# K of the second attention transposed in place, in one ring of eight tiles, in a two-attention kernel on one Trainium2 core

## The chip, the cores and the metric

The kernel runs on one core of one Trainium2 chip. The core has a matrix engine (PE, whose weight loads are listed apart as PEld), a vector engine (DVE), an engine for activations (ACT), a general one (POOL) and a sequencer (SP) that issues all transfers here. 16 DMA engines move the data between device memory and the on-chip memory, which has 128 partitions. Engines run their own instructions in order and wait for each other through semaphores. The metric is the time of one execution on the device in microseconds (us); lower is better.

## What is computed

Two attention blocks, A and B, over the same shapes of x (16 sequences of 32 tokens, width 1024; all data bf16), with the outputs side by side. A has 4 heads of K and V that 8 query heads share, B has 32 of its own. Each K and V head holds 1024 positions of 128 numbers per sequence.

```python
def _B_ref(x, k_cache, v_cache, wq, wo):
    q = (x @ wq).reshape(B, Sq, H, Dh).transpose(0, 2, 1, 3)
    scores = jnp.einsum("bhqd,bhkd->bhqk", q, k_cache) * (Dh ** -0.5)
    p = _softmax(scores, axis=-1)
    o = jnp.einsum("bhqk,bhkd->bhqd", p, v_cache)
    return o.transpose(0, 2, 1, 3).reshape(B, Sq, H * Dh) @ wo
# A the same, with k and v repeated 8 times along the head axis
return jnp.concatenate([a, b], axis=-1)
```

B's K and V are 134 MB each, A's 17 MB each, and every byte of them is read once.

## The kernel before

**Steps.** The work is cut into 128 steps (NIT). Each step t handles one "quad" of B (two sequences by two heads, `quadB_all`, L940) and about one quad of A (`quadA_all`, L958). A quad of B needs two K tiles and two V tiles of 512 KB (t_ = 0 and 1, one for each sequence); a new K and V tile of A (256 KB each) comes every second quad. Between them stand the projections to queries (L598, L616, with weights wq), the output projections (L680, weights wo) and their sums (L691, L694).

**One quad of B.** Two K tiles land in `KB_sb` (`st_dmaK`, L740, issue at L750). DVE transposes each in blocks of 32 x 32 (as float32 words, so that pairs of bf16 stay together) into `KBt_sb` (`st_ktrB`, L782, instruction at L785). PE makes the scores from it in 32 small matmuls (L827), split in four groups so that others can come between. DVE finds the maximum (L837), ACT takes the exponential (L850), PE transposes the result (L862), ACT or DVE copies that out of PE's accumulators (L526), PE multiplies by V (PV, L892), and the norm (L908 or L909), a last transpose (L914) and a copy follow. A's quads take the same course with a K that PE transposes (L776, scores L806, PV L884).

**Buffers.** With NKB_SLOTS = 2, `KB_sb` has 2 * NKB = 4 landing tiles of 512 KB and `KBt_sb` another 4 for the transposed ones: two steps of each. V has a ring of three steps (NVB_SLOTS = 3, six tiles, issue at L763). A's K and V (L745, L757) have two tiles each, the weights wq (L579) and wo (L652, L662) one place for each piece.

**Order.** `Prog.add` takes the operations in program order and derives from their reads and writes what each must wait for: a transfer into a tile waits for whoever last read or wrote it. Then `list_schedule` (L223) sets the order of every engine by simulating the program with the constants at the top of the file: each operation becomes ready when all it waits for is done, and among the ready ones an engine takes what can start first, with preference for what has the longest rest of its own step behind it, less 3 us for each step (STEP_US). SP's queue, too, is put in this order: a transfer is not placed earlier than SP_AHEAD = 5 us before the simulated DMA engines can take it (L318 to L319, L350 to L351). A K transfer is simulated with DMA_FIRST = 1.4 us, its bytes at 4096 per 0.159 us and engine, and DMA_LAST = 0.8 us. On the chip the order within each engine is fixed, and every instruction waits on its semaphores in that order.

**Where K is asked for.** In step t, right behind each of the two transposes, the transfer for the same half of step t + NKB = t + 2 is added (L942 to L945); its landing tile is the one that the transpose has just read. The transpose in turn writes the pair `t % 2` of `KBt_sb`, which the scores of step t - 2 must have left. V of step t + 2 is added behind the transposes (L946, L947); its place is the one of step t - 1, whose PV must be done. K of steps 0 and 1 is asked for before the first step (L987 to L997).

Of the kernel before, what the change touches and what calls it, by code (L numbers as in the profile page):

```python
# [10 lines left out]
BF = mybir.dt.bfloat16  # L11
F32 = mybir.dt.float32
# [2 lines left out]
HOOK = None  # L15
SCHED = True
NVB_SLOTS = 3
NKB_SLOTS = 2
LAZY_PER_STEP = 100
LAZY_DELAY = 4  # L20
A_STEPS_FRAC = 0.97
# [409 lines left out]
def build(nc, pa, pb, out):  # L431
    P = 128
# [5 lines left out]
    Dh = pa["k"].shape[3]  # L438
# [8 lines left out]
    NVB = NVB_SLOTS  # L447
    NKB = NKB_SLOTS
    HqA = pa["wq"].shape[1] // Dh
# [6 lines left out]
    NIT = NSB * NG * 8  # L456
# [7 lines left out]
    pr = Prog()  # L464
    stack = contextlib.ExitStack()
    with stack:
        def sb(name, shape, dt):
            return stack.enter_context(nc.sbuf_tensor(name, shape, dt))
# [14 lines left out]
        QR = sb("QR", [P, 2, 4, 2, Dh], BF)  # L483
# [2 lines left out]
        acc = sb("acc", [P, 2, NG, D], F32)  # L486
        OTA_sb = sb("OTA_sb", [P, 2, HS, P], BF)
        OTB_sb = sb("OTB_sb", [P, 2, MS, P], BF)
        KB_sb = sb("KB_sb", [P, 2 * NKB, 16 * Dh], BF)
        KBt_sb = sb("KBt_sb", [P, 2, 2, 16 * Dh], BF)  # L490
        VB_sb = sb("VB_sb", [P, NVB, 2, 2, NCH, Dh], BF)
        KA_sb = sb("KA_sb", [P, 2, NCH, Dh], BF)
        VA_sb = sb("VA_sb", [P, 2, NCH, Dh], BF)
# [14 lines left out]
        if HOOK is not None:  # L508
# [4 lines left out]
               reads=["zeros"], writes=["ident"], name="c1")  # L513
        pr.add("pool", lambda g: g.memset(z32[:], 0.0), writes=["z32"], name="c0")
        pr.add("pool", lambda g: g.affine_select(id32[:], z32[:], [[1, P]], ALU.not_equal, 1.0, base=0, channel_multiplier=-1),
               reads=["z32"], writes=["id32"], name="c1")
# [203 lines left out]
        def mk_quadB(t):  # L720
            q = Quad()
            q.pi = 1
            q.t = t
            q.m = t // (NG * 4)
            q.G = (t // 4) % NG
            jb = t % 4
            q.bp = jb // 2
            q.hp = jb % 2
            q.b0 = 4 * q.G + 2 * q.bp
            q.h0 = q.m * MS + 2 * q.hp  # L730
            q.kvslot = t % 2
            q.krslot = t % NKB
            q.vslot = t % NVB
            q.first_of_group = (jb == 0)
            q.last_of_group = (jb == 3)
            q.qid = ("B", t)
            q.kid = ("B", t)
            return q

        def st_dmaK(q, t_=None):  # L740
            if q.pi == 0:
                if not q.kv_new:
                    return
                sl = q.kvslot
                pr.add("sp", lambda e: e.dma_start(KA_sb[:, sl, :, :], pa["k"][q.b, q.s].rearrange("(p c) d -> p c d", c=NCH)),  # L745
                       writes=[("KA", sl)], dma_key=f"ka{sl}", name="ka_dma", dur=Sk * Dh * 2, wtag={("KA", sl): q.kid})
            else:
                sl = (2 * q.t + t_) % (2 * NKB)
                ksrc = pb["k"][q.b0 + t_, q.h0:q.h0 + 2].rearrange("hh (p s) d -> (hh p) (s d)", s=16)
                pr.add("sp", lambda e: e.dma_start(KB_sb[:, sl, :], ksrc), writes=[("KB", sl)], dma_key=f"kb{sl}", name="kb_dma", dur=2 * Sk * Dh * 2, wtag={("KB", sl): q.kid})  # L750

        def st_dmaV(q):
            if q.pi == 0:
                if not q.kv_new:
                    return
                sl = q.kvslot
                pr.add("sp", lambda e: e.dma_start(VA_sb[:, sl, :, :], pa["v"][q.b, q.s].rearrange("(p c) d -> p c d", c=NCH)),  # L757
                       writes=[("VA", sl)], dma_key=f"va{sl}", name="va_dma", dur=Sk * Dh * 2, wtag={("VA", sl): q.kid})
            else:
                sl = q.vslot  # L760
                for t_ in range(2):
                    vsrc = pb["v"][q.b0 + t_, q.h0:q.h0 + 2].rearrange("hh (p c) d -> p hh c d", c=NCH)
                    pr.add("sp", lambda e, t_=t_, vsrc=vsrc: e.dma_start(VB_sb[:, sl, t_, :, :, :], vsrc), writes=[("VB", sl, t_)],  # L763
                           dma_key=f"vb{sl}_{t_}", name="vb_dma", dur=2 * Sk * Dh * 2, wtag={("VB", sl, t_): q.kid})
# [15 lines left out]
                 wtag={("KTA", sl): q.kid})  # L780

        def st_ktrB(q, t_):  # L782
            sl = q.kvslot
            rs = (2 * q.t + t_) % (2 * NKB)
            pr.add("dve", lambda e: e.transpose(KBt_sb[:, sl, t_, :].bitcast(F32), KB_sb[:, rs, :].bitcast(F32)),  # L785
                   reads=[("KB", rs)], writes=[("KBt", sl, t_)], name="KBt_tr", rtag={("KB", rs): q.kid}, wtag={("KBt", sl, t_): q.kid})

        s_rr = [0]

# [5 lines left out]
        def st_scores(q):  # L795
            q.vS = SBuf(s_rr[0] % 2)
            s_rr[0] += 1
            q.vP, q.vPT, q.vst, q.vO = Virt("P"), Virt("PT"), Virt("stat"), Virt("O")
            q.vbt, q.vbo = Virt("bank"), Virt("bank")
            vS = q.vS  # L800
            if q.pi == 0:
                sl = q.kvslot
                qt = QT_sb[:, q.s % 2]

                for u in range(2):
                    pr.add("pe", lambda e, u=u: e.matmul(ps_s[:, vS.idx, u, :], qt[:, q.b, q.hh0:q.hh0 + 4, :].rearrange("p a q -> p (a q)"),  # L806
                                                         KTA_sb[:, sl, u * 512:(u + 1) * 512], start=True, stop=True),
                           reads=[("QT", q.s % 2, q.hh0 + a) for a in range(4)] + [("KTA", sl)], writes=vS.res, name="scoresA", dur=0.225,
                           tag="A%d" % q.t, rtag=dict([(("QT", q.s % 2, q.hh0 + a), q.s) for a in range(4)] + [(("KTA", sl), q.kid)]))
            else:  # L810
                sl = q.kvslot
                gp = (q.m * NG + q.G) % 2

                def e_s(e, fp):
                    last = None
                    if True:
                        f, pd = fp // 2, fp % 2
                        o0 = f * 64 + pd
                        for t_ in range(2):
                            a = 2 * q.bp + t_  # L820
                            for hh in range(2):
                                cg = 2 * t_ + hh
                                for g2 in range(2):
                                    rg = 2 * hh + g2
                                    lhsT = QR[32 * rg:32 * rg + 32, gp, a, q.hp, o0:o0 + 63:2]
                                    rhs = KBt_sb[32 * rg:32 * rg + 32, sl, t_, :].rearrange("p (s x) -> p s x", s=16)[:, :, o0:o0 + 63:2]
                                    last = e.matmul(ps_s[32 * cg:32 * cg + 32, vS.idx, g2, :].rearrange("p (s j) -> p s j", s=16), lhsT, rhs,  # L827
                                                    start=(fp == 0), stop=(fp == 3), tile_position=(32 * rg, 32 * cg))
                    return last
                for fp_ in range(4):  # L830
                    pr.add("pe", lambda e, fp_=fp_: e_s(e, fp_), reads=[("QR", gp, 2 * q.bp), ("QR", gp, 2 * q.bp + 1), ("KBt", sl, 0), ("KBt", sl, 1)],
                           writes=vS.res, name="scoresB", dur=0.275, tag="B%d" % q.t,
                           rtag={("QR", gp, 2 * q.bp): (q.m, q.G), ("QR", gp, 2 * q.bp + 1): (q.m, q.G), ("KBt", sl, 0): q.kid, ("KBt", sl, 1): q.kid})

        def st_max(q):
            vS, vst = q.vS, q.vst
            pr.add("dve", lambda e: e.tensor_reduce(stat[:, vst.idx, 0:1], ps_s[:, vS.idx, :, :], AXIS.XY, ALU.max, negate=True),  # L837
                   writes=vS.res + [vst], name="max")
# [27 lines left out]
        def st_pev(q, eng=None):  # L866
            vPT, vb = q.vPT, q.vbt
            evac(lambda: PT_sb[:, vPT.idx, :, :].rearrange("p c q -> p (c q)").bitcast(F32), lambda: bank(vb), reads=[], writes=[vb, vPT],
                 name="PT_ev", eng=eng)
# [63 lines left out]
        quadsB = [mk_quadB(t) for t in range(NIT)]  # L933
# [6 lines left out]
        def quadB_all(q):  # L940
            t = q.t
            for t_ in range(2):  # L942
                st_ktrB(q, t_)
                if t + NKB < NIT:
                    st_dmaK(quadsB[t + NKB], t_)  # L945
            if t >= 1 and t - 1 + NVB < NIT:  # L946
                st_dmaV(quadsB[t - 1 + NVB])  # L947
            st_scores(q)
            st_max(q)
            st_exp(q)  # L950
            st_ptr(q)
            st_pev(q)
            st_pv(q)
            st_recip(q)
            st_norm(q)
            st_otr(q)
# [30 lines left out]
        for t_ in range(2):  # L987
            st_dmaK(quadsB[0], t_)
        st_dmaV(quadsB[0])
        for t in range(2, min(NKB, NIT)):  # L990
            st_dmaK(quadsB[t], 0)
            st_dmaK(quadsB[t], 1)
        st_dmaK(quadsA[newA[0]])
        st_dmaV(quadsA[newA[0]])
        if NIT > 1:
# [86 lines left out]
        if SCHED:  # L1082
            pr = pr.list_schedule()
# [41 lines left out]
```

## Time and profile before

| | |
|---|---|
| time, median of 3 runs | 903.89 us (901.42 to 905.68) |
| span of the profiled execution | 902.6 us |
| PE busy | 836.3 us (93%) |
| PE weight loads busy | 481.8 us (53%) |
| DVE busy | 745.3 us (83%) |
| ACT busy | 610.8 us (68%) |
| bytes moved | 341.67 MB, mean 379 GB/s |
| DVE transposes of B's K (L785) | 256, mean 1231 ns |
| B's K transfers (L750) | 256 of 512 KB, median 9.2 us from issue to landing |
| B's V transfers (L763) | 256 of 512 KB, median 8.1 us |
| mean granted PE clock | 0.985 of full speed |

The span goes from the first to the last instruction of one profiled execution. "Busy" is the time in which an engine has at least one instruction in it; matmuls overlap and their ends are modelled, so a full PE is not at its peak rate. SPq is SP's queue. In lists of waits, a line such as "DVE KBt_sb L785 <- DMA KB_sb" says that the engine sat idle before an instruction of line 785 and what ended that. In the rows over 40 slices each digit is the busy share of one fortieth of the span in tenths. In the timeline a line has start, length, engine, line, operation, output and inputs, and in brackets the idle time before it.

### The profile page before, as it was taken

What the parts mean: (1) busy time and instruction counts of PE and PEld (TensorE: products, weight loads), DVE (VectorE), ACT (ScalarE), POOL (GpSimd) and SP (SyncE); (2) the same over time, 40 slices, a digit from 0 to 9 for tenths busy, and PEclk for the clock granted to TensorE, in tenths of its full rate; (3) what the DMA queues carried; (4) which work ended last, traced back from release to release, by engine and by line L of the source; (5) the groups of instructions that cost most, each with busy time, mean ns of one, the idle gap of its engine ahead of it and who ended that gap; (6) DMA issues with size and microseconds to landing.
All of it is one profiled execution on the core that took longest, in us unless ns stands there. A gap on an engine that the chain in (4) does not pass through costs nothing.

```text
span 902.6 us, 29455 instructions
## 1 busy us (share of the span) xinstructions
PE 836.3 (93%) x12864; PEld 481.8 (53%) x12864; DVE 745.3 (83%) x1057; ACT 610.8 (68%) x1384; POOL 1.1 (0%) x8
## 2 busy tenths in 40 slices
PE   6999999999899999999999998999998988999886
PEld 4365555555555555555545455555555554555453
DVE  0578897888887999689887899878979788798885
ACT  3477886677666776676776466776867666586763
POOL 0000000000000000000000000000000000000000
PEclk9999999999999999999999999999999999999999
DMA  9999999999999999999999999999999999999994
GB/s 325 383 389 393 386 385 392 390 393 383 392 387 389 393 380 388 380 386 376 387 385 391 394 369 389 388 393 370 388 387 391 392 391 367 344 393 393 393 377 170
DMA packets 153984, 341.67 MB, mean 379 GB/s; under 512 B 12544, under 2 KB 28928, under 8 KB 153856
## 3 DMA queue, kind: packets, MB, share of 16 engines
q1 hardware_dynamic: 153856, 339.79, 100.6%
q8 instruction: 102, 1.67, 0.8%
q14 instruction: 26, 0.21, 0.1%
HBM read 337.64 MB, written 2.10 MB: 376 GB/s over the span
## 4 chain that ended last, share of the span: by engine, by line
PE 48%; DMA 23%; DVE 19%; ACT 8%; SPq 1%; issue 1%; ACTq 0%; DVEq 0%
DMA KB_sb<-in_B_k_cache_dram 21%; PE ps_s L827 10%; PE ps_g L862 9%; DVE stat L837 8%; DVE KBt_sb L785 8%; PE ps_g L680 6%; ACT P_sb L850 5%; PE ps_g L892 4%; PE ps_g L598 4%; PE ps_g L884 4%; PE ps_g L616 3%; PE ps_s L806 3%; PE ps_g L776 2%; ACT PT_sb L526 1%; PE ps_g L914 1%
## 5 line engine op out<-in xcount | busy, mean ns | idle before, releaser
L785 DVE STREAM_TRANSPOSE KBt_sb<-KB_sb 128x1024 f32<-128x1024 f32 x256 | 311.8, 1231 | 42.5 <-DMA KB_sb<-in_B_k_cache_dram 40.4
L837 DVE TENSOR_REDUCE stat<-ps_s 128x1 f32<-128x1024 f32 x256 | 304.7, 1209 | 50.7 <-PE ps_s L827 34.3
L850 ACT ACTIVATE P_sb<-ps_s,stat 128x1024 bf16<-128x1024 f32 x256 | 285.8, 1119 | 51.5 <-DVE stat L837 50.0
L862 PE MATMUL ps_g<-id,P_sb 128*128 128x128 f32 x1024 | 177.0, 300 | 13.0 <-ACT P_sb L850 4.7
L862 PEld LDWEIGHTS ps_g<-id,P_sb 128*128 128x128 f32 x1024 | 150.5, 207 | 54.9 <-issue 11.1
L827 PE MATMUL ps_s<-KBt_sb,QR 32*32 32x512 bf16 x4096 | 157.2, 399 | 19.5 <-ACT P_sb L850 10.9
L526 ACT COPY PT_sb<-ps_g 128x512 f32<-128x512 f32 x234 | 134.9, 591 | 59.5 <-PE ps_g L862 58.3
L908 ACT ACTIVATE O_sb<-ps_g,stat 128x128 bf16<-128x128 f32 x199 | 71.4, 370 | 63.0 <-PE ps_g L892 32.4
L806 PE MATMUL ps_s<-KTA_sb,QT_sb 128*128 128x512 bf16 x256 | 91.5, 388 | 6.0 <-ACT P_sb L850 5.6
L827 PEld LDWEIGHTS ps_s<-KBt_sb,QR 32*32 32x32 bf16 x4096 | 49.3, 90 | 81.1 <-ACT P_sb L850 17.8
L892 PE MATMUL ps_g<-VB_sb,PT_sb 128*32 128x128 bf16 x4096 | 91.1, 224 | 1.4 <-ACT PT_sb L526 0.9
L892 PEld LDWEIGHTS ps_g<-VB_sb,PT_sb 128*32 128x32 bf16 x4096 | 60.2, 97 | 48.7 <-issue 29.2
L884 PE MATMUL ps_g<-VA_sb,PT_sb 128*128 128x128 bf16 x1024 | 78.8, 220 | 1.8 <-ACT PT_sb L526 0.7
L884 PEld LDWEIGHTS ps_g<-VA_sb,PT_sb 128*128 128x128 bf16 x1024 | 61.6, 98 | 28.2 <-issue 8.5
L616 PE MATMUL ps_g<-wq_sb,xT_sb 128*128 128x512 bf16 x256 | 71.4, 386 | 2.9 <-DMA wq_sb<-in_B_wq_dram 2.8
L680 PE MATMUL ps_g<-woB_sb,OTB_sb 128*128 128x512 bf16 x256 | 68.7, 381 | 4.4 <-ACT OTB_sb L526 1.8
L598 PE MATMUL ps_g<-xT_sb,wq_sb 128*128 128x512 bf16 x256 | 72.0, 385 | 0.3
L680 PE MATMUL ps_g<-woA_sb,OTA_sb 128*128 128x512 bf16 x256 | 63.0, 380 | 1.3 <-DVE OTA_sb L526 1.0
L914 PE MATMUL ps_g<-ident,O_sb 128*128 128x128 bf16 x256 | 51.8, 224 | 3.0 <-ACT O_sb L908 2.0
L850 ACT ACTIVATION_READ_ACCUMULATOR P_sb<-ps_s,stat 128x1 f32 x256 | 51.8, 202 | 0.0
L526 ACT COPY OTA_sb<-ps_g 128x64 f32<-128x64 f32 x114 | 24.7, 216 | 36.7 <-PE ps_g L914 36.1
L691 DVE TENSOR_TENSOR acc<-acc,ps_g 128x512 f32<-128x512 f32 x64 | 41.2, 675 | 8.1 <-PE ps_g L680 7.6
(41 smaller groups left out, 537.5 us busy)
## 6 DMA issues: line engine op xcount, KB each, us to landing
VB_sb<-in_B_v_cache_dram SPq DMA_DIRECT2D x256, 512.0 KB, 8.1
KB_sb<-in_B_k_cache_dram SPq DMA_DIRECT2D x256, 512.0 KB, 9.2
KA_sb<-in_A_k_cache_dram SPq DMA_DIRECT2D x64, 256.0 KB, 7.7
VA_sb<-in_A_v_cache_dram SPq DMA_DIRECT2D x64, 256.0 KB, 8.1
wq_sb<-in_B_wq_dram SPq DMA_DIRECT2D x32, 256.0 KB, 8.6
wq_sb<-in_A_wq_dram SPq DMA_DIRECT2D x32, 256.0 KB, 8.8
woB_sb<-in_B_wo_dram SPq DMA_DIRECT2D x32, 256.0 KB, 9.2
woA_sb<-in_A_wo_dram SPq DMA_DIRECT2D x32, 256.0 KB, 9.1
```

The source lines that it names most:

```text
L526: return e.copy(dst, src) if hasattr(e, "activation") else e.tensor_copy(dst, src)
L598: last = e.matmul(bank(v)[:, 0:tn], wq_sb[:, 0, j, hc * Dh:(hc + 1) * Dh], xT_sb[:, 0, j, t0:t0 + tn], start=(j == 0), stop=(j == DJ - 1))
L616: last = e.matmul(bank(v)[:, 0:CW], xT_sb[:, 1, j, G * P:(G + 1) * P], wq_sb[:, 1, j, :], start=(j == 0), stop=(j == DJ - 1))
L680: last = e.matmul(bank(v)[:, 0:OUTW], OT[:, gp, hh, :], wo_[:, hh, oh * OUTW:(oh + 1) * OUTW], start=(hh == 0), stop=(hh == nh - 1))
L785: pr.add("dve", lambda e: e.transpose(KBt_sb[:, sl, t_, :].bitcast(F32), KB_sb[:, rs, :].bitcast(F32)), reads=[("KB", rs)], writes=[("KBt" ...
L806: pr.add("pe", lambda e, u=u: e.matmul(ps_s[:, vS.idx, u, :], qt[:, q.b, q.hh0:q.hh0 + 4, :].rearrange("p a q -> p (a q)"), KTA_sb[:, sl, ...
L827: last = e.matmul(ps_s[32 * cg:32 * cg + 32, vS.idx, g2, :].rearrange("p (s j) -> p s j", s=16), lhsT, rhs, start=(fp == 0), stop=(fp == 3 ...
L837: pr.add("dve", lambda e: e.tensor_reduce(stat[:, vst.idx, 0:1], ps_s[:, vS.idx, :, :], AXIS.XY, ALU.max, negate=True), writes=vS.res + [v ...
L850: return e.activation(dst, src, ACTF.Exp, bias=stat[:, vst.idx, 0:1], scale=1.0, accum_out=stat[:, vst.idx, 1:2])
L862: last = e.transpose(bank(vb)[:, m * P:(m + 1) * P], p32[:, m:Sk // 2:NPK], id32[:])
L884: last = e.matmul(bank(vb)[:, 0:Dh], ptc_of(vPT, c, 0, P), VA_sb[:, kvs, c, :], start=(c == 0), stop=(c == NCH - 1))
L892: last = e.matmul(bank(vb)[32 * a:32 * a + 32, 0:Dh], ptc_of(vPT, c, 32 * a, 32 * a + 32), VB_sb[:, kvs, a // 2, a % 2, c, :], start=(c == ...
```

## The change

`KBt_sb` goes. `KB_sb` becomes one ring of NKB = 8 tiles (the same 8 x 512 KB as the two buffers before), and step t uses tiles 2t and 2t + 1 modulo 8, so four steps fit. DVE transposes each tile onto itself, and the scores read the tile there. So a tile is held from the issue of its transfer to the end of its scores; the transfer for step t + 4 waits for the scores of step t, and the transpose waits for nothing but its landing. The transfers for t + NKB // 2 = t + 4 are added behind the scores. In steps 0 and 1 the transfers for steps 2 and 3 are added before the scores (their tiles are unused until then), and the loop ahead of the first step that would have asked for further K tiles (empty with NKB = 2) is gone. The tags ("T", q.kid) only check, while the program is put together, that the scores name a tile in its transposed state.

```diff
-NKB_SLOTS = 2
+NKB_SLOTS = 8
...
-        KB_sb = sb("KB_sb", [P, 2 * NKB, 16 * Dh], BF)
-        KBt_sb = sb("KBt_sb", [P, 2, 2, 16 * Dh], BF)
+        KB_sb = sb("KB_sb", [P, NKB, 16 * Dh], BF)
...
-            q.kvslot = t % 2
-            q.krslot = t % NKB
+            q.ks = [(2 * t + t_) % NKB for t_ in range(2)]
...
         def st_ktrB(q, t_):
-            sl = q.kvslot
-            rs = (2 * q.t + t_) % (2 * NKB)
-            pr.add("dve", lambda e: e.transpose(KBt_sb[:, sl, t_, :].bitcast(F32), KB_sb[:, rs, :].bitcast(F32)),
-                   reads=[("KB", rs)], writes=[("KBt", sl, t_)], name="KBt_tr", rtag={("KB", rs): q.kid}, wtag={("KBt", sl, t_): q.kid})
+            sl = q.ks[t_]
+            pr.add("dve", lambda e: e.transpose(KB_sb[:, sl, :].bitcast(F32), KB_sb[:, sl, :].bitcast(F32)),
+                   writes=[("KB", sl)], name="KBt_tr", rtag={("KB", sl): q.kid}, wtag={("KB", sl): ("T", q.kid)})
...
-                                    rhs = KBt_sb[32 * rg:32 * rg + 32, sl, t_, :].rearrange("p (s x) -> p s x", s=16)[:, :, o0:o0 + 63:2]
+                                    rhs = KB_sb[32 * rg:32 * rg + 32, q.ks[t_], :].rearrange("p (s x) -> p s x", s=16)[:, :, o0:o0 + 63:2]
...
             for t_ in range(2):
                 st_ktrB(q, t_)
-                if t + NKB < NIT:
-                    st_dmaK(quadsB[t + NKB], t_)
             if t >= 1 and t - 1 + NVB < NIT:
                 st_dmaV(quadsB[t - 1 + NVB])
+            if t in (0, 1) and t + 2 < NIT:
+                for t_ in range(2):
+                    st_dmaK(quadsB[t + 2], t_)
             st_scores(q)
+            if t + NKB // 2 < NIT:
+                for t_ in range(2):
+                    st_dmaK(quadsB[t + NKB // 2], t_)
             st_max(q)
...
-        for t in range(2, min(NKB, NIT)):
-            st_dmaK(quadsB[t], 0)
-            st_dmaK(quadsB[t], 1)
```

More of the change, by code (lines that the diff above doesn't have):

```diff
@@ L747, in st_dmaK @@
             else:
-                sl = (2 * q.t + t_) % (2 * NKB)
+                sl = q.ks[t_]
                 ksrc = pb["k"][q.b0 + t_, q.h0:q.h0 + 2].rearrange("hh (p s) d -> (hh p) (s d)", s=16)
@@ L782, in st_ktrB @@
         def st_ktrB(q, t_):
-            sl = q.kvslot
-            rs = (2 * q.t + t_) % (2 * NKB)
-            pr.add("dve", lambda e: e.transpose(KBt_sb[:, sl, t_, :].bitcast(F32), KB_sb[:, rs, :].bitcast(F32)),
-                   reads=[("KB", rs)], writes=[("KBt", sl, t_)], name="KBt_tr", rtag={("KB", rs): q.kid}, wtag={("KBt", sl, t_): q.kid})
+            sl = q.ks[t_]
+            pr.add("dve", lambda e: e.transpose(KB_sb[:, sl, :].bitcast(F32), KB_sb[:, sl, :].bitcast(F32)),
+                   writes=[("KB", sl)], name="KBt_tr", rtag={("KB", sl): q.kid}, wtag={("KB", sl): ("T", q.kid)})
         s_rr = [0]
@@ L810, in st_scores @@
             else:
-                sl = q.kvslot
                 gp = (q.m * NG + q.G) % 2
@@ L830, in st_scores @@
                 for fp_ in range(4):
-                    pr.add("pe", lambda e, fp_=fp_: e_s(e, fp_), reads=[("QR", gp, 2 * q.bp), ("QR", gp, 2 * q.bp + 1), ("KBt", sl, 0), ("KBt", sl, 1)],
+                    pr.add("pe", lambda e, fp_=fp_: e_s(e, fp_), reads=[("QR", gp, 2 * q.bp), ("QR", gp, 2 * q.bp + 1), ("KB", q.ks[0]), ("KB", q.ks[1])],
                            writes=vS.res, name="scoresB", dur=0.275, tag="B%d" % q.t,
-                           rtag={("QR", gp, 2 * q.bp): (q.m, q.G), ("QR", gp, 2 * q.bp + 1): (q.m, q.G), ("KBt", sl, 0): q.kid, ("KBt", sl, 1): q.kid})
+                           rtag={("QR", gp, 2 * q.bp): (q.m, q.G), ("QR", gp, 2 * q.bp + 1): (q.m, q.G), ("KB", q.ks[0]): ("T", q.kid), ("KB", q.ks[1]): ("T", q.kid)})
         def st_max(q):
```

## The prediction

> **What bounds the kernel now.** I read the two rows of the 40 slices first: they tell whether the transfers leave room.
>
> ```profile
> DMA  9999999999999999999999999999999999999994
> GB/s 325 383 389 393 386 385 392 390 393 383 392 387 389 393 380 388 380 386 376 387 385 391 394 369 389 388 393 370 388 387 391 392 391 367 344 393 393 393 377 170
> ```
>
> The transfers run at about 390 GB/s almost all the time; the first and last slices and a few in between are lower. I take 390 as the rate of a stretch in which nothing holds the transfers up. 341.67 MB (the page's count) at 390 GB/s is 876.1 us, 26.5 less than the span of 902.6. Where those 26.5 lie is shown by the busy time in four stretches (columns: stretch, length, then busy time and instructions of PE, its weight loads, DVE, ACT and POOL, granted clock, DMA share, GB/s):
>
> ```profile
> 0.00:10.00 10.00, 4.82 (x30) 2.69 (x30) 0.00 (x0) 3.80 (x4) 1.15 (x8) 1.00 0.79 251
> 10.00:860.00 850.00, 800.12 (x12283) 460.91 (x12283) 715.45 (x1014) 584.90 (x1328) 0.00 (x0) 0.99 1.03 386
> 860.00:889.00 29.00, 24.04 (x444) 13.86 (x436) 25.37 (x38) 16.96 (x40) 0.00 (x0) 1.00 0.98 370
> 889.00:902.60 13.60, 7.28 (x116) 4.31 (x116) 4.45 (x10) 5.12 (x13) 0.00 (x0) 0.85 0.12 45
> ```
>
> Length times (390 - GB/s)/390 gives the time lost in each: 3.6 us, 8.7, 1.5 and 12.0. So no change of buffers can win more than about 10.2 us while transfers stream, and what it wins in the tail it wins by work done earlier. PE is nearly full as well (800 of 850 us in the long stretch), so the kernel has two limits close together. A smaller time at either needs the other to follow.
>
> Next the waits of the engines and those of SP, which issues every transfer in order (columns: us in total, times, longest):
>
> ```profile
> DVE KBt_sb L785 <- DMA KB_sb<-in_B_k_cache_dram: 40.4, 39, 8.6
> ```
>
> ```profile
> SPq L763 <- PE ps_g L892: 136.7, 69, 7.4
> SPq L750 <- DVE KBt_sb L785: 115.2, 77, 5.2
> ```
>
> K of the second attention is the late transfer: after the start, engines wait for it 40.4 us, for A's K 0.7 us, for the weights some 9 us, and PE never stands on a V tile. And SP stands before the K transfer (L750) because its landing tile still has to be transposed. Summed over releasers SP stands 158.0 us at L750, 224.9 at L763 (B's V) and 552.4 in all.
>
> **The change, part by part.** The instructions are the same in number: 256 transposes, 256 K transfers, 4096 score matmuls. What differs is what each waits for.
>
> *The transpose in place.* It cost 311.8 us / 256 = 1231 ns and nothing in the trace shows one that writes over its input. The nearest row that does, on the same engine, is the accumulation at L691 (acc<-acc,ps_g, 512 elements, 675 ns), against 682 ns for a copy of 512 elements to another tile (PT_sb at L526 on DVE): no difference. I take 0. The ends: -7 ns each by that pair of rows (1.8 us of DVE time) and +16 ns by the longest of the 256, 1247 ns (4.1 us). DVE is busy 745.3 of 902.6 us, so its idle time covers either; where DVE stands on the chain there is no cover, but the transposes hold 8% of the chain of waits, which makes 0.3 us of the 4.1.
>
> *The transpose no longer waits for the scores of two steps before* (its target pair was free only then). No instruction falls away; a transpose can now stand up to three steps ahead in DVE's order.
>
> *The K transfer gets a longer lead.* First and last scores start at 31.4 and 889.8 us, 128 steps: 6.76 us a step. Before, the transfer for step t+2 is let go by the transposes of step t and needed by those of t+2: two steps, 13.5 us, against a landing of 9.2 us median and 13.7 at most. So the margin is 4.3 us in the median and below nothing at worst, which agrees with the 39 waits. After, it is let go by the scores of t and needed by the transposes of t+4: four steps less about one from transpose to scores, 20.3 us, margin 6.6 us even at the longest landing. So the 40.4 us should mostly go. What then is late next is V: let go by PV of t, needed at PV of t+3, three steps or 20.3 us against 12.9 at most. It isn't late either as long as landing times stay as they are.
>
> *The added wait.* The K transfer now waits for PE (scores, L827) in place of DVE. Behind it in SP's queue stand the V tiles, A's K and V and the weights. PE's scores of t come some microseconds after the transposes of t, but two steps more are in hand, so I count SP's 158.0 us at L750 as the part that can be given back: 158.0/552.4 = 29% of its standing. Applied to the 10.2 us lost while streaming that is 2.9 us; the other end is all of them, 10.2. And the lower end is below nothing, since the planner reorders all SP, PE and DVE work and PE has only 6% to spare: 0.5% of the span, -4.5. **I take 4 us won**, near the 2.9, as that has a row.
>
> The Trainium skill (DMA: Bandwidth & Descriptors, "Where 436 GB/s comes from") puts two ceilings on such a transfer, about 358 GB/s on the memory side and 435 at the ports; by the first these bytes would need an estimated 954 us, more than the whole span, and the trace's 389 to 394 GB/s contradicts it, while by the second an estimated 785 us, a hundred microseconds of room. The trace never shows a slice above 394, so the sum goes by 390.
>
> *The tail.* From the end of the chain of waits:
>
> ```profile
> 878.51 3.63 PE ps_g L680 x16
> 882.14 1.11 PE ps_s L827 x32
> 883.25 0.02 issue
> 883.27 1.23 DVE stat L837
> 884.50 4.53 DVE KBt_sb L785 x4
> 889.03 0.06 DVE stat L901
> 889.09 1.13 PE ps_s L827 x23
> ```
>
> The transposes of the last two steps (4.53 us) stand on the chain, between two score blocks. Their K tiles were issued here:
>
> ```profile
> 874.89 5.49 SPq L750 DMA_DIRECT2D KB_sb<-in_B_k_cache_dram  x4
> 880.43 2.81 SPq L697 DMA_DIRECT2D out_dram<-acc  x2
> 885.23 0.90 SPq L763 DMA_DIRECT2D VB_sb<-in_B_v_cache_dram  x2
> ```
>
> With a landing of some 9 us they arrive at 884 to 889. After, the scores of four steps before let them go, some two steps or 13 us earlier, and the transposes fit into DVE's idle time at 875 to 877 and 882. Then the last V tile is next: issued at 885.23, landed about 889 (the rate falls from 295 to 12 GB/s at 890), and its PV ran in the block that starts at 893.94. So at most 4.9 us are to be had before V is late, and 4.5 of them are the transposes'. The other end is 0 (PE's order unchanged). **I take 4 us won.**
>
> *The start.* Two more steps of K (2.1 MB, 5.4 us at 390 GB/s) have no tile to wait for and can be queued about 14 us into the span; before, K of step 2 is issued at 32.28. The second weight chunk, issued at 19 to 31 us, is then up to 5.4 us later; the chain stands there now (wq_sb, 9.49 us from 26.14) and PE waited 7.6 us for B's weights. Against it the same bytes are missing later. Ends 0 and +5.4; **I take 1 us lost**, nearer to nothing, as the steps that follow are limited by the total of bytes.
>
> *Four more semaphores* are waited for at the end by SP, all long done: 0.
>
> **Sum**: -4 - 4 + 1 = -7 us. The profiled execution's span is 902.6 us, 1.3 below the median of the runs, 903.89, which I take as what lies around it. 895.6 + 1.3 gives **897 us**. Less than 0.5% (899.4 to 908.4) can hardly be told from no change.
>
> **Rivals.**
>
> *The transfers are the limit, or the longer lead isn't used* (chance 0.24, 903 us). For it: 389 GB/s from 40 to 240 us, and a planner that lets SP run only SP_AHEAD = 5 us ahead of its own model of the transfers: if K is queued no earlier, or K's waits only become V's (224.9 us of SP at L763 stay), what falls away is the tail or nothing: -4 + 1 to 0, and some of it lost to order. Against it: the stretches below 375 GB/s, many of which begin with SP at L750 (5.2 us there at 520 to 526, then 324 GB/s).
>
> *DVE stands before K tiles that nobody needs yet* (0.28, 916 us, slower). DVE works in order, and the planner, whose constants give a K transfer 1.4 + 1.27 + 0.8 = 3.5 us from issue to landing, plus at most 5 us of transfers before it, where the chip's median is 9.2 and its longest 13.7, now may place a transpose three steps ahead. Such a one holds up the ready maximum behind it. The trace has the pattern at 140.21: 3.56 us of waiting, four transposes in a row of 5.13 us, and only then the maximum at 145.27. DVE is busy up to 88.8 us of 100 (140 to 240), with 4.5 us of K waits; it decides from about 12 us of K waits per 100, 2.7 times today's, when nothing is left to absorb them. At three times (121 us, 13.4 per 100) the excess is 1.4 us per 100, 12.6 us in all: 916. Against it: the longer lead makes most tiles land before their turn.
>
> *The forecast* has 0.48, with its own range 887 to 899: 889.3 when all 10.2 us and 4.4 of the tail are won, less 2 for the spread of the runs.
>
> Chances: faster 0.48, within 0.5% 0.24, slower 0.28. The range for 8 in 10 goes from 887 to 916, since the slower case holds too much to be left out.
>
> **What would show it.** Right: DVE's wait for KB_sb far below 40.4 us, SP at L750's counterpart below 158 us, the slices at 367, 344, 369 and 370 GB/s filled, the last K issued some two steps before the last V, and no four transposes on the last part of the chain; the transpose still near 1231 ns. Wrong: DVE's K waits of 40 us or more, PE waiting for VB_sb, weights waited for longer than 9 us, a transpose above 1350 ns, or the same GB/s row with the waits under other names.

## The result, and the profile after

The changed kernel takes 897.8 us (median of 4 runs, 896.76 to 897.89) where the kernel before, beside it, takes 904.75 (901.42 to 905.68). The ratio is 0.9925, with a 95% interval of 0.9903 to 0.9948: 0.75% faster. The span of the profiled execution went from 902.6 to 896.0 us.

The page's two rows over the 40 slices, for the changed kernel:

```profile
DMA  9999999999999999999999999999999999999994
GB/s 324 386 387 394 395 391 385 382 396 389 388 387 390 395 395 378 385 394 395 394 365 388 392 395 396 379 386 394 393 387 372 392 395 394 396 394 395 397 368 145
```

Seventeen of the 40 slices are now at 394 to 397 GB/s, where one reached 394 before. Of the slices between the first and the tail that lie below 375, two are left (365 and 372), where there were four, down to 344; those four are now at 394 to 396. The last slice is emptier (145, it was 170). The busy times in the same four stretches as before (length; PE, weight loads, DVE, ACT and POOL; granted clock, DMA share, GB/s; the last stretch is shorter as the span is):

```profile
0.00:10.00 10.00, 5.04 (x29) 2.91 (x30) 0.00 (x0) 3.79 (x4) 1.14 (x8) 1.00 0.79 251
10.00:860.00 850.00, 782.87 (x12257) 458.99 (x12423) 717.99 (x1016) 594.14 (x1357) 0.00 (x0) 1.00 1.04 390
860.00:889.00 29.00, 23.71 (x404) 13.70 (x402) 21.42 (x29) 13.28 (x31) 0.00 (x0) 0.86 0.74 266
889.00:896.00 7.00, 2.22 (x28) 0.69 (x17) 1.37 (x2) 0.58 (x2) 0.00 (x0) 0.94 0.10 37
```

By the prediction's measure, length times (390 - GB/s)/390, the long stretch now loses nothing (8.7 us before), the two last ones 9.2 + 6.3 = 15.5 us (13.5 before), the first the same 3.6. (A GB/s of rounding is 2.2 us in the long stretch; from the unrounded bytes it loses 0.9 us now and 9.5 before.) That the difference, -6.7 us, is nearly that of the spans, -6.6, proves nothing, as the bytes are the same; it only says in which stretch the time went. The waits (us in total, times, longest), first DVE's for K, then SP's before K transfers, now at L748, and before V transfers, now at L761:

```profile
DVE KB_sb L782 <- DMA KB_sb<-in_B_k_cache_dram: 28.6, 24, 7.6
```

```profile
SPq L761 <- PE ps_g L888: 88.0, 36, 5.4
SPq L761 <- PE ps_s L823: 84.9, 34, 7.1
SPq L748 <- PE ps_g L679: 1.9, 3, 1.4
```

SP's standing at the K transfer is all but gone: 7.2 us over all releasers, from 158.0. Before V it stands 213.2 us (224.9), in all 314.8 (552.4). But DVE still waits 28.6 us for K. Two groups of the page tell why and settle another question (in the first, 1228 is the mean of one transpose in ns, in the second, 12.1 is the median from issue to landing in us):

```profile
L782 DVE STREAM_TRANSPOSE KB_sb<-KB_sb 128x1024 f32<-128x1024 f32 x256 | 309.8, 1228 | 30.3 <-DMA KB_sb<-in_B_k_cache_dram 28.6
```

```profile
KB_sb<-in_B_k_cache_dram SPq DMA_DIRECT2D x256, 512.0 KB, 12.1
```

A transpose onto its own input takes 1228 ns where the one into another tile took 1231. And a K transfer now takes 12.1 us to land, not 9.2: transfers are asked for earlier and stand longer in the queue. Adding up size times (landing - issue) over all transfers between 20 and 860 us, and dividing by 840, gives 4.30 MB under way in the mean, 3.31 before. From landing to the start of the transpose the median is 0.7 us, as before (0.6). So the longer lead has gone into a fuller queue and not into tiles that lie ready. And not all of it is used: a K transfer goes out 7.2 us (median) after the end of the scores that let it go, where before it went out 0.8 us after the transpose that did. From issue to the start of the tile's transpose there are now 12.7 us, 10.1 before (7.2 and 12.7 together are 19.9, close to the 20.3 us of lead that the prediction reckoned).

Where in the course of the work the 6.6 us came from is shown by the first score matmul of some steps in both traces:

| us | start to step 8 | 8 to 120 | 120 to 124 | 124 to the end |
|---|---|---|---|---|
| before | 91.4 | 758.6 | 23.5 | 29.0 |
| changed | 88.4 | 749.5 | 28.8 | 29.3 |

The stream wins 12.1 us by step 120, and the last eight steps give 5.6 back. Going by the first PV of step 120 in place of its first scores gives much the same, 13.0 won and 6.5 given back.

### The profile page after: what moved, and what is told of

Its sections match the earlier page's. It is cut to its first block, busy times and chain, and to the rows that moved or that the text cites. A ratio compares the mean times of both kernels' runs of the same rounds, so it can differ in the third digit from the quotient of the medians.

```text
span 896.0 us, 29282 instructions
## 1 busy us (share of the span) xinstructions
PE 813.8 (91%) x12693; PEld 476.3 (53%) x12864; DVE 740.8 (83%) x1047; ACT 611.8 (68%) x1394; POOL 1.1 (0%) x8
## 4 chain that ended last, share of the span: by engine, by line
PE 51%; DMA 18%; DVE 16%; ACT 9%; SPq 3%; issue 3%; DVEq 0%; ACTq 0%
PE ps_s L823 11%; PE ps_g L858 9%; DMA KB_sb<-in_B_k_cache_dram 8%; PE ps_g L679 8%; DVE stat L833 7%; DVE KB_sb L782 5%; ACT P_sb L846 5%; PE ps_g L888 5%; DMA wq_sb<-in_A_wq_dram 4%; PE ps_g L880 4%; PE ps_g L597 4%; PE ps_g L615 3%; DMA VA_sb<-in_A_v_cache_dram 3%; PE ps_s L803 2%; PE ps_g L774 2%
## 5 line engine op out<-in xcount | busy, mean ns | idle before, releaser
L782 DVE STREAM_TRANSPOSE KB_sb<-KB_sb 128x1024 f32<-128x1024 f32 x256 | 309.8, 1228 | 30.3 <-DMA KB_sb<-in_B_k_cache_dram 28.6
L846 ACT ACTIVATE P_sb<-ps_s,stat 128x1024 bf16<-128x1024 f32 x256 | 286.4, 1121 | 66.8 <-DVE stat L833 63.7
L858 PE MATMUL ps_g<-id,P_sb 128*128 128x128 f32 x1024 | 174.0, 296 | 14.0 <-ACT QR L525 4.5
L823 PE MATMUL ps_s<-KB_sb,QR 32*32 32x512 bf16 x4096 | 161.9, 400 | 15.7 <-ACT P_sb L846 10.7
L904 ACT ACTIVATE O_sb<-ps_g,stat 128x128 bf16<-128x128 f32 x173 | 63.0, 372 | 58.9 <-PE ps_g L888 35.3
L823 PEld LDWEIGHTS ps_s<-KB_sb,QR 32*32 32x32 bf16 x4096 | 46.6, 89 | 74.6 <-ACT P_sb L846 17.5
L615 PE MATMUL ps_g<-wq_sb,xT_sb 128*128 128x512 bf16 x223 | 67.2, 389 | 5.5 <-issue 2.5
L803 PE MATMUL ps_s<-KTA_sb,QT_sb 128*128 128x512 bf16 x182 | 66.5, 384 | 5.5 <-ACT P_sb L846 1.5
L597 PE MATMUL ps_g<-xT_sb,wq_sb 128*128 128x512 bf16 x232 | 65.8, 380 | 5.4 <-issue 1.9
L679 PE MATMUL ps_g<-woB_sb,OTB_sb 128*128 128x512 bf16 x229 | 62.0, 380 | 4.9 <-issue 2.3
L525 ACT CAST QR<-ps_g 128x256 bf16<-128x256 f32 x117 | 43.7, 382 | 18.4 <-PE ps_g L637 14.3
## 6 DMA issues: line engine op xcount, KB each, us to landing
KB_sb<-in_B_k_cache_dram SPq DMA_DIRECT2D x256, 512.0 KB, 12.1
wq_sb<-in_B_wq_dram SPq DMA_DIRECT2D x32, 256.0 KB, 10.1
```

The lines of the kernel that those rows point to most:

```text
L525: return e.copy(dst, src) if hasattr(e, "activation") else e.tensor_copy(dst, src)
L597: last = e.matmul(bank(v)[:, 0:tn], wq_sb[:, 0, j, hc * Dh:(hc + 1) * Dh], xT_sb[:, 0, j, t0:t0 + tn], start=(j == 0), stop=(j == DJ - 1))
L615: last = e.matmul(bank(v)[:, 0:CW], xT_sb[:, 1, j, G * P:(G + 1) * P], wq_sb[:, 1, j, :], start=(j == 0), stop=(j == DJ - 1))
L679: last = e.matmul(bank(v)[:, 0:OUTW], OT[:, gp, hh, :], wo_[:, hh, oh * OUTW:(oh + 1) * OUTW], start=(hh == 0), stop=(hh == nh - 1))
L782: pr.add("dve", lambda e: e.transpose(KB_sb[:, sl, :].bitcast(F32), KB_sb[:, sl, :].bitcast(F32)), writes=[("KB", sl)], name="KBt_tr", rta ...
L846: return e.activation(dst, src, ACTF.Exp, bias=stat[:, vst.idx, 0:1], scale=1.0, accum_out=stat[:, vst.idx, 1:2])
```

## The experiments

**Theory**: the longer lead lets SP ask for K whenever the queue has room, so the transfers stream at 390 GB/s in place of 386. **Rivals**: the gain comes from transposes that need not wait for old scores; or any new order from the planner moves the time by so much. Each run is compared with the kernel before on the same chip, and with the changed kernel by the two ratios to the kernel before. Line numbers in diffs are left out; unless it says otherwise, the edit is to the changed kernel.

**The old wait back, the lead kept.**

```diff
-                   writes=[("KB", sl)], name="KBt_tr", rtag={("KB", sl): q.kid}, wtag={("KB", sl): ("T", q.kid)})
+                   writes=[("KB", sl), ("KX", q.t % 2, t_)], name="KBt_tr", rtag={("KB", sl): q.kid}, wtag={("KB", sl): ("T", q.kid)})
...
-                    pr.add("pe", lambda e, fp_=fp_: e_s(e, fp_), reads=[("QR", gp, 2 * q.bp), ("QR", gp, 2 * q.bp + 1), ("KB", q.ks[0]), ("KB", q.ks[1])],
+                    pr.add("pe", lambda e, fp_=fp_: e_s(e, fp_), reads=[("QR", gp, 2 * q.bp), ("QR", gp, 2 * q.bp + 1), ("KB", q.ks[0]), ("KB", q.ks[1]), ("KX", q.t % 2, 0), ("KX", q.t % 2, 1)],
```

> The changed kernel, with one wait of before put back: the transposes of step t again wait for the scores of step t-2 (a marker that the transposes write and the scores read). The ring of eight and the longer lead of the K transfers stay. Theory (the longer lead lets the transfers stream without dips): nothing is lost, 898 us, ratio to before 0.992 to 0.995, and 389 GB/s or more from 10 to 860 us. Rival (what helps is that DVE may transpose ahead): back to 904 us, ratio 0.998 to 1.002. A third rival (any new order from the planner moves the time by some tenths of a per cent): anywhere from 0.988 to 1.004, without a relation to GB/s.

Measured: 896.16 us, ratio 0.9924 (0.9904 to 0.9943), 4.33 MB under way. The stretch from 10 to 860 us:

```profile
10.00:860.00 850.00, 782.16 (x12258) 461.22 (x12425) 715.37 (x1010) 596.21 (x1363) 0.00 (x0) 0.99 1.04 390
```

390 GB/s at the end of the row, and the ratio of the changed kernel: with the old wait, nothing is lost. The freedom to transpose ahead is worth nothing here that the interval (0.2% each way) would show.

**The old lead, the wait left out.**

```diff
                 st_ktrB(q, t_)
+                if t + 2 < NIT:
+                    st_dmaK(quadsB[t + 2], t_)
...
-            if t in (0, 1) and t + 2 < NIT:
-                for t_ in range(2):
-                    st_dmaK(quadsB[t + 2], t_)
...
-            if t + NKB // 2 < NIT:
-                for t_ in range(2):
-                    st_dmaK(quadsB[t + NKB // 2], t_)
```

The transpose also writes a marker ("KY", q.t, t_), and the transfer reads ("KY", q.t - 2, t_), so that it waits for the transpose of two steps before.

> The changed kernel with the lead of before: the transfer for step t+2 is asked for behind the transpose of step t and waits for it, as in the kernel before. The ring of eight stays, so the transposes may still run ahead of the scores. Theory: the gain goes, 902 to 905 us, ratio 0.997 to 1.002, DVE's wait for K about 40 us as before, about 3.3 MB under way in the mean, 386 GB/s from 10 to 860 us. Rival (transposing ahead): 898 us, ratio 0.992. Third rival (order alone): anywhere between.

Measured: 901.4 us, ratio 0.9986 (0.997 to 1.0002), 3.37 MB under way. The wait of DVE, SP's wait before K, and the long stretch:

```profile
DVE KB_sb L782 <- DMA KB_sb<-in_B_k_cache_dram: 39.6, 40, 7.4
```

```profile
SPq L748 <- DVE KB_sb L782: 120.4, 79, 5.2
```

```profile
10.00:860.00 850.00, 777.78 (x12170) 460.76 (x12340) 721.78 (x1023) 587.52 (x1330) 0.00 (x0) 1.00 1.04 388
```

The waits of the kernel before are back (40.4 and 115.2 us there), in spite of the ring of eight tiles, and the gain is nearly gone. The rate is 388 GB/s and not the 386 expected; the profiled execution was 1.8 us faster than the median. These two runs tell the two parts of the change apart: it is the lead.

**Rings of six and of four tiles.**

```diff
-NKB_SLOTS = 8
+NKB_SLOTS = 6
...
-            if t in (0, 1) and t + 2 < NIT:
+            if t in (0, 1) and t + 2 < min(NIT, NKB // 2):
```

> The changed kernel with a ring of six tiles: the transfer for step t+3 waits for the scores of step t. The lead is three steps less one, 13.5 us, against a landing of 9.2 us before and 12.1 after. Theory: between the two kernels, 899 to 902 us, ratio 0.994 to 0.998. Rival (transposing ahead, which needs only two or three steps of tiles): 898 us, ratio 0.992. Third rival (order alone): anywhere from 0.988 to 1.004.

> The changed kernel with a ring of four tiles, half the memory of the kernel before: the transfer for step t+2 waits for the scores of step t. The lead is two steps less one, 6.8 us, less than the shortest usual landing of 9 us. Theory: K is late in nearly every step: scores, issue 0.5 us, landing 9.2 us, two transposes 2.5 us and the next scores 1.1 us make 13.3 us or more for two steps, all in a row, so any delay adds up: 910 to 940 us, ratio 1.007 to 1.04, DVE's wait for K above 80 us. Rival (transposing ahead matters, the lead doesn't): about 904 us or less.

Measured, six: 898.31 us, ratio 0.9949 (0.9928 to 0.9969), 389 GB/s, landing 10.2 us, 3.70 MB under way. Four: 924.01 us, ratio 1.023 (1.0201 to 1.0258), landing 8.1 us, 3.03 MB under way. The slices of the ring of four:

```profile
GB/s 324 383 382 386 350 389 391 391 341 378 370 390 392 394 388 370 393 391 340 388 389 392 391 365 385 388 393 383 346 387 363 394 346 387 310 392 389 388 398 171
```

and what SP waits for longest there, in total:

```profile
SPq L748 <- PE ps_s L823: 130.6, 62, 4.8
```

Now the K transfer does stand behind the scores, and the row has holes down to 310 GB/s (378 from 10 to 860 us). Four, six and eight tiles give 378, 389 and 390 GB/s and 1.023, 0.995 and 0.9925. The step from four to six is clear; six and eight cannot be told apart, since their intervals overlap, and the 898.31 us of six lie as near to the rival's 898 as to the theory's 899. Three steps of lead bring nearly all of the gain. DVE's wait for K with four tiles was 49.3 us, not the 80 expected: the tiles land faster there, with fewer under way.

**Half of B's V bytes left out**, in the kernel before and in the changed one, with the planner's view of it unchanged:

```diff
+                    nh = 2 if q.t < NVB else 1
-                    pr.add("sp", lambda e, t_=t_, vsrc=vsrc: e.dma_start(VB_sb[:, sl, t_, :, :, :], vsrc), writes=[("VB", sl, t_)],
+                    pr.add("sp", lambda e, t_=t_, vsrc=vsrc, nh=nh: e.dma_start(VB_sb[:, sl, t_, 0:nh, :, :], vsrc[:, 0:nh]), writes=[("VB", sl, t_)],
```

> The kernel before, in which from step 3 on only the first of the two heads of each V tile of B is loaded, half its bytes (65.5 MB less, 168 us at 390 GB/s); the other half keeps the values of the first three steps, so the output of B is not the reference's. The order of all engines is the same, since the planner still counts the whole tile. Theory (the transfers set the pace while they stream): the time falls well below 904 us, to what the order and PE allow, 840 to 885 us, and DVE's wait for K falls from 40 us to under 10, since K lands in less than 7 us. Rival (PE sets the pace): 895 us or more.

> The same half of B's V bytes left out in the changed kernel (its output of B is not the reference's either). Theory: with transfers that land in time the lead of K is worth nothing, so this one and the kernel before with the same bytes left out lie within 0.4% of each other (4 us), in 840 to 885 us. Rival (the changed order of DVE and PE is itself worth 0.75%): the changed kernel stays 6 to 8 us ahead.

Measured: 891.13 us (ratio 0.9865, 0.9842 to 0.9889) from the kernel before, 888.41 (0.9837, 0.9812 to 0.9863) from the changed one. The long stretch of each, first the one from the kernel before:

```profile
10.00:860.00 850.00, 782.25 (x12344) 465.16 (x12516) 722.98 (x1037) 596.15 (x1356) 0.00 (x0) 1.00 0.91 317
```

```profile
10.00:860.00 850.00, 788.16 (x12373) 464.88 (x12540) 721.44 (x1026) 597.80 (x1369) 0.00 (x0) 0.99 0.90 319
```

At 317 and 319 GB/s the transfers have room, and yet the time falls by some 12 and 8 us only (ratios 1 to 0.9865, 0.9925 to 0.9837), between what the two sides expected. The engines in their order need some 888 to 891 us even so; PE is busy 782 to 788 of the 850 us, but which engine holds the time there was not taken apart. So a second limit lies some 8 us below the time of the changed kernel, and by this estimate a better prefetch could hardly win more than that with these orders. With room, the two kernels differ by 2.7 us in place of 7. From step 8 to 120 they take 744.0 and 742.6 us, so of the 9.1 us that the change won there, 1.4 remain with room, and the rest needs the transfers to be tight.

**Another order and nothing else**, LOOK = 0.30 in place of 0.35, in both kernels:

```diff
-LOOK = 0.35
+LOOK = 0.30
```

> The kernel before with LOOK 0.30 in place of 0.35, as was done with the changed kernel: a new order and nothing else. Theory (the lead of K decides, order alone moves 2 to 3 us): 900 to 907 us, ratio 0.996 to 1.004, DVE's wait for K 35 us or more, some 3.3 MB under way. Rival (order alone gives such gains too): 897 us or less.

> The changed kernel with one constant of the planner moved a little (LOOK 0.30 in place of 0.35), which changes the order within the engines and nothing else. It measures how much a new order alone moves the time. Theory (the lead decides): within 3 us of the changed kernel, 895 to 901 us, 389 GB/s or more from 10 to 860 us. Rival (order alone decides): 5 us or more away.

Measured: from the kernel before, 901.98 us, ratio 0.9982 (0.9968 to 0.9996), 388 GB/s, 3.51 MB under way; from the changed one, 895.23, ratio 0.9911 (0.9888 to 0.9934), 390 GB/s, 4.49 MB. The one other order that was tried moves either by 1 to 3 us; the distance between them, 6.8 us, stays. The other runs agree that order alone is not the cause: all five other kernels with the lead of the changed kernel or a step more (old wait back, LOOK, ten K tiles, and the last two below) lie at 0.991 to 0.995, the two with the lead of before at 0.998 to 0.999. One kernel in between does not fit as well: six K tiles with four steps of V, below, have three steps of lead and lie at 0.998. The wait of DVE for K was 29.1 us in the first, below the 35 expected, as short as in the changed kernel and without its gain.

**The memory shared out otherwise**: six K tiles and four steps of V, or ten and two.

```diff
-NVB_SLOTS = 3
-NKB_SLOTS = 8
+NVB_SLOTS = 4        # or 2
+NKB_SLOTS = 6        # or 10
...
-            if t in (0, 1) and t + 2 < NIT:
+            if t in (0, 1) and t + 2 < min(NIT, NKB // 2):    # or: if t in (0, 1, 2) and t + 2 < NIT
```

> The changed kernel with two K tiles less and two V tiles more: ring of six for K, four steps for V, in the same memory. In the changed kernel SP stands 213 of 315 us before V transfers. Theory (what counts is that something can always be asked for): SP's standing before V falls below half, the mean under way stays at 4.0 to 4.5 MB, 390 GB/s or more from 10 to 860 us, 895 to 899 us, ratio 0.990 to 0.995. Rival (K's lead alone counts, V never is late): as with a ring of six alone, 898 to 900 us, ratio 0.995.

> The changed kernel with the memory divided the other way: ring of ten for K (the transfer for step t+5 waits for the scores of t), two steps for V in place of three. K's lead grows by a step, V's falls to two steps, 13.5 us, against a landing of 10.9 us. Theory (the tile with the shortest lead over its landing sets the pace): V becomes late, PE waits for VB_sb more than 10 us where it was 1.1, 899 to 912 us. Rival (K's lead is what counts): 898 us or less.

Measured: six and four, 901.14 us, ratio 0.9979 (0.9963 to 0.9996), 388 GB/s, 3.66 MB under way, SP standing 269.0 us before V, DVE waiting 34.8 us for K. Ten and two, 897.84, ratio 0.9935 (0.9915 to 0.9956), 389 GB/s, 4.00 MB, PE waiting only 2.0 us for VB_sb. I was wrong on both: the first lies above both ranges, in the second the rival came true. The first is no better than six K tiles with three steps of V, rather 2.8 us worse, which is no more than a new order can bring: a V tile there lies 15.2 us between landing and PV (median, for the second tile of a step; 8.2 with three steps, 5.2 in the changed kernel, 0.8 with two). The added tiles stood full, and the mean under way didn't grow. With two steps of V, V lands just in time and hardly anyone waits. The reason that I see, and have not shown by itself: a place for V comes free only behind a long chain (scores, maximum, exponential, PV), a place for K behind its scores. Of the three ways to share out this memory, eight and three or ten and two cannot be told apart, and six and four is the worst.

**A planner that knows the landing better.**

```diff
-DMA_FIRST = 1.4
+DMA_FIRST = 4.4
```

> The changed kernel with one constant of the planner nearer to what the chip shows: DMA_FIRST 4.4 in place of 1.4 us, so that its K transfers take 6.5 us from issue to landing plus the queue (the chip: 12.1 in the changed kernel). Theory (part of DVE's 28.6 us of waiting for K comes from transposes placed ahead of their landing): DVE's wait for K below 20 us, 893 to 898 us. Rival (K lands when the full queue brings it, whatever the order): the wait stays at 22 to 32 us and the time at 895 to 900 us.

Measured: 898.14 us, ratio 0.9937 (0.9915 to 0.9959), 389 GB/s, 4.24 MB under way. DVE's wait for K:

```profile
DVE KB_sb L782 <- DMA KB_sb<-in_B_k_cache_dram: 18.3, 23, 2.6
```

A third of the wait went, as the theory said, and the time stayed where the rival had it: 10 us less of DVE's standing before K bring nothing here that the interval (0.2% each way) would show.

**Transposes preferred.**

```diff
-PRIO_BONUS = {}
+PRIO_BONUS = {"KBt_tr": 6.0}
```

> The changed kernel, in which the planner prefers the transposes of K by two steps' worth (PRIO_BONUS of 6 us for KBt_tr): DVE takes a landed tile as soon as it can. It asks whether the transposes on the last part of the chain, late in DVE's order, cost the tail the 4 us that the prediction had counted as won there. Theory: the last transposes leave the chain, the span after 860 us shortens by 2 to 5 us, 893 to 897 us. Rival (DVE then stands before tiles that nobody needs yet and the maxima come later): 900 to 915 us, DVE's wait for K above 35 us.

Measured: 898.84 us, ratio 0.9946 (0.9921 to 0.9971), 387 GB/s, 3.51 MB under way, DVE waiting 21.3 us for K. Neither side: the time is that of the changed kernel within the interval. Why it is, with less under way and a lower rate, stays open. In its chain the last transposes are gone, and this stands there instead:

```profile
883.07 0.37 SPq L761
883.44 0.04 issue
883.48 5.22 DMA VB_sb<-in_B_v_cache_dram
888.70 0.14 issue
888.83 1.10 PE ps_g L888 x64
```

The last V tile is next late, and the end comes no sooner (37.1 us of the span lie behind 860, 36.0 in the changed kernel).

## Why the prediction was right, and where its steps were not

The sum (-7 us) and the time (897) were met, but its terms were not: by the transfers' account the stream gave 4.7 us more than counted, the tail 6.0 less, and the 1 us at the start was not lost. That these errors nearly cancel is luck. What was right is the cause: the lead of the K transfers.

*While transfers stream: counted 4 us, measured 8.7.* The mechanism was right: SP's standing before K was what made the holes, since the run with the old lead brings holes and waits back and the one with the old wait doesn't. The size was too small, because I gave K only its share of SP's standing, 29%. SP works in order, so a K transfer that doesn't stand lets those behind it go too: at A's V (L757, then L755) SP's standing fell from 66.8 to 12.0 us; it is 69.5 with the old lead and 13.2 with the old wait. The ceiling on this term, 10.2 us, had no ground either: 390 GB/s is not the rate of transfers that nothing holds up, since slices of up to 397 came. And the gain does not lie in the four deep dips alone, since the median of the slices rose as well, from 388 to 391.5 GB/s.

*"So the 40.4 us should mostly go": wrong.* 28.6 stayed. The margin of 6.6 us was wrong in two places. I took a K transfer as issued when the scores let it go, but it goes out 7.2 us later in the median. As SP's standing before K is by chance also 7.2 us, but over all 256 transfers together, it is not the tile that keeps a transfer but its place in SP's queue, behind others. That much of the rival "the longer lead isn't used" was true: a third of the 20.3 us isn't. And I took the landing time of before, which in the fuller queue grew by 2.9 us. So the time from issue to transpose grew by 2.6 us and the landing took it all. The wait is also a poor measure: 18.3 us of it (planner told of longer landings) goes with 898.1 us, 31.7 (old wait back) with 896.2, and 29.1 in the kernel before with another order with 902.0.

*The tail: counted 4 us won, measured 2.0 lost* by the transfers' account, 5.6 by the steps'. K of the last two steps did arrive earlier, at 870.9 to 874.7 us. But the planner put the transposes late in DVE's order, between sums of the output projection, so that they start 2.0 to 3.6 us after landing (1.0 to 1.4 before):

```profile
872.53 0.69 DVE acc L693
873.22 3.41 DVE KB_sb L782 x3
876.62 0.58 DVE acc L693
877.26 0.41 issue
877.67 0.69 DVE acc L693
```

I had them move into DVE's idle time, as if the order had been free. My bound was misread too: the last V tile of the kernel before landed at 891.0 us, not about 889, so 2.9 us and not 4.9 lay between it and its PV. With half of V left out these K tiles land 9 us and more before their transposes start, and the stretch from step 124 to the end still takes 30.2 us (29.0 in the kernel before, 29.3 in the changed one). So the end from step 124 on is set by the order of the engines and not by K's landing. Of the 5.3 us lost from step 120 to 124, 2.6 are there as well with half of V left out (26.1 against 23.5 us); what makes the other half stays open.

*The start: counted 1 us lost, measured none.* K of step 2 was issued at 32.27 us, as before (32.28); the planner did not put it ahead of the weights. Step 8 gives no clear sign: its first scores come 3.0 us sooner than before, its last PV ends 1.0 us later.

*The transpose in place: counted 0, measured -3 ns each.* Right. (311.8 us / 256 is 1218 ns, not 1231: 311.8 is the time in which DVE has at least one transpose in it, 1231 the page's mean of one, and transposes in a row overlap a little. The term stays 0.)

*The rivals.* That the transfers are the limit anyway was wrong in its reason: they had holes, and the holes went. But a second limit is near, as I had said of PE: with 65.5 MB less the changed kernel still needs 888.4 us, though no run shows that it is PE that holds it. That DVE stands before K tiles that nobody needs yet did not come: its waits went down, and with transposes preferred to an extreme the time stayed at 898.8. That 887, the lower end of the range, lies so near to 888.4 is chance, as it came from winning all of the 10.2 us and 4.4 of the tail. The upper end was wider than needed.

*Its own signs.* SP's standing before K, the four slices, the last K (17.5 us ahead of the last V) and the time of a transpose came as said for a right prediction. DVE's wait did not fall far below 40.4 us, and transposes still stand on the last part of the chain. Two signs of being wrong came as well: PE waits 1.1 us for VB_sb, and the engines wait 11.8 us for the weights wq in place of 8.9. Neither kept the time from its forecast.

The fastest run that moves all bytes is the changed kernel with LOOK = 0.30, 895.23 us. It beats the changed kernel by no more than a chance order brings.

## What to carry to other kernels

When transfers are the limit and still have holes, look at the queue that issues them: what it stands on, and for how long, says which buffer turns over too late. More buffers help as long as they are empty and on their way, so look at when a transfer is issued and not only at when its buffer comes free. The bytes under way told more here than the waits of the engine that uses them: from 3.0 to 3.4 MB the ratio was 1.023 to 0.999, from 3.5 to 3.7 it was 0.998 to 0.995, from 4.0 to 4.5 it was 0.994 to 0.991. They are no exact measure: 3.51 MB go with 0.998 once and with 0.995 once. And before counting on a gain, ask what the engines would need with transfers out of the way: here the second limit was some 8 us below the time reached, and at the end of this program the order of the engines, not the arrival of K, decided.

## What the runs showed of the hardware

In this kernel the time to land follows what is under way: 3.03, 3.31, 3.70 and 4.30 MB in the mean go with medians of 8.1, 9.2, 10.2 and 12.1 us for a K tile. 4.30 MB at 390 GB/s are 11.0 us, an estimate by which nearly all of the 12.1 us is standing in line. And the DVE transpose of 128 x 1024 words onto its own input runs as fast as one into another tile (1228 against 1231 ns).
